# Batch 0's last query block: two key groups mirrored by DMA, and two weight loads put behind waits of the loading queue

## The chip, the cores and the metric

The kernel runs on one core of a Trainium2 chip. The metric is the device time of one execution in microseconds (us), as the median of several runs. A profiled execution has a time of its own, and a span: from its first to its last instruction.

The core has five engines that run side by side, each through its own list of instructions in order: PE (TensorE, matmuls), DVE (VectorE), ACT (ScalarE), POOL (GpSimd) and SP (SyncE). POOL and SP do hardly anything here but issue DMAs. An instruction waits until the semaphores that it needs have their values, and everything behind it on its engine waits with it.

## What is computed

A gated attention without softmax is followed by an MLP mixer, for 8 batches of 3008 rows of 256 channels (z has 64):

```
scores = z @ z.T / 3008                      # 3008 x 3008, symmetric
x      = u * (relu(scores)**2 @ v)
h      = relu(x.T @ w_tok1) @ w_tok2         # over the rows: 3008 -> 256 -> 3008
y      = x + h.T
out    = y + relu(y @ w_ch1) @ w_ch2         # over the channels: 256 -> 1536 -> 256
```

Inputs and output are float32 in memory; the kernel works in bf16 with float32 accumulation.

## The kernel before

**Tiles.** The queries of a batch are cut into 6 blocks (512 columns, the last 448), the keys into 6 groups of 4 tiles of 128. A group of a block, written (b, q, g), is made in two units. A unit is a pair of score matmuls (L440) of 64 rows each, which share the array, into a PSUM pair of banks `sc`; an ACT instruction (L478: relu and scale) into a tile `at`; and a DVE instruction that squares it in place (L486). Later PE multiplies the group with v (L677, called value matmuls here) into accumulators of the block. There are 6 buffers of `at`, and a buffer is written anew only when all that read its last content have finished.

**Mirrors.** Since the scores are symmetric, group (b, g, q) is the transpose of (b, q, g). `direct_block` (L276) says which groups are computed. In batches 1 to 7 that is those with g >= q; the others are mirrors: when both units of (b, q, g) are squared, SP issues one transposing DMA (`flip`, L542) from its `at` into a buffer `fl`, and the value matmuls of (b, g, q) read `fl`. Such an `at` has two users, the block's own value matmuls and the DMA, and its layout is another one (a form 128x4x256 of L478 and L486). In batch 0, MIRROR = 6 makes every group direct: all 36 are computed, and no mirror is made. `key_order` (L286) puts the groups of a block in order.

**Order.** The program is written out by a planner that runs while the kernel is built. It keeps a model of each engine (when it is free, what each step costs), and at each turn writes the step that fits best: a unit's scores, half a group's value matmuls, or a piece of the mixer. What it writes is each engine's fixed order; the chip then keeps to it, whatever the true times are. A step pushed to an engine (`push`, L339) has a room condition. For a mirror that is a free `fl` buffer and `flips_fit` (L536): before the mixer fewer than MIRRORS = 6 buffers of `fl` may be in use; batch 0's six v tiles lie in `fl` buffers too.

**SP** issues all transposes in the order written: of z (`turn_z`, L140 and L144), of u (`turn_u`, L233), of x (`turn_x`, L855) and the mirrors (L546).

**POOL** issues all loads in the order written: z, v, u, w_tok1 (L241), w_tok2 (L251), w_ch1 in two parts (L258) and w_ch2 in two parts (L263). Loads of weights and of u go into buffers of their own and mostly wait for nothing but an old load of their semaphore lane, so POOL runs ahead of the work. Where it must not, `after(column)` (L121) writes a copy of one column of a tile in POOL's order: POOL goes on when that tile is there. `recent[0]` is the tile that was last planned to be written.

**When loads are asked for.** `at_group(n, f)` (L1483) calls f when the planner takes up the n-th group of value matmuls (n counts 6 a block, so block (0,4) begins at 24). The list `items` (L1626) has 24 loads, spread over groups 7 to 33 in its order: v of batch 1, w_tok1, w_tok2, four parts of w_ch, and u (1,0) and u (1,1). So w_tok2's last part is asked for at group 26, w_ch1 at 28 and 29, w_ch2 at 30 and 31. `ask_w_ch` (L1605) also plans the weight sums: when the last part is asked for, four DVE instructions (`sum_weights`, L1611) are pushed that read w_ch2.

## Time and profile before

| | us |
|---|---|
| median of 3 runs | 1116.72 (1116.61 to 1116.90) |
| the profiled execution | 1117.16 |
| its span | 1115.0 |
| PE busy | 1104.5 (99% of the span) |
| DVE busy | 761.9 (68%) |
| ACT busy | 673.0 (60%) |
| POOL busy | 152.2 (14%) |
| block (0,0) ends, (0,1) begins on PE | 24.9 |
| value matmuls of (0,5) begin, with 448 columns | 75.85 |
| batch 0's mixer begins on PE (L900) | 99.65 |

The granted TensorE clock is 0.999 of full speed over the span. A row of the timeline reads: start, duration, engine, line, operation, output and input tiles, how many instructions are merged, and the idle time before them with what ended it. Matmuls overlap in the pipe, so the pace is read from starts, not from durations. [...]

### The profile page before, as it was taken

The numbers are of one execution on the slowest core, as the hardware profiler recorded it, in microseconds if no ns is written. First come the engines' busy times: TensorE is split into PE (matmuls) and PEld (weight loads), VectorE is DVE, ScalarE is ACT, GpSimd is POOL, SyncE is SP. The second block draws the span as 40 slices with busy tenths as digits, with TensorE's granted clock in tenths as the row PEclk, the third lists the DMA queues.
The fourth block names the chain that finished last, engine by engine and source line by source line (L and its number), as shares of the span: only waits on it lengthen the run. The fifth ranks groups of instructions, "written<-read, shape, count | busy, mean of one in ns | idle before, by whom it ended". The sixth has DMA issues, their size and how long they took to land.

```text
span 1115.0 us, 26448 instructions
## 1 busy us (share of the span) xinstructions
PE 1104.5 (99%) x10714; PEld 666.6 (60%) x10788; DVE 761.9 (68%) x1587; ACT 673.0 (60%) x840; POOL 152.2 (14%) x387
## 2 busy tenths in 40 slices
PE   9999999999999999999999999999999999999998
PEld 3555654666447665676545765567654576545676
DVE  7887875676756867568656676566756677655676
ACT  8997585545755467555665456664666636743464
POOL 5401000221002210022100221003210021000000
PEclk9999999999999999999999999999999999999999
DMA  9999485997859988598694997869888697574222
GB/s 173 189 167 185 105 165 110 189 172 145 165 117 193 168 132 183 95 210 168 139 179 96 204 155 153 164 104 219 141 156 153 127 200 145 120 153 84 66 65 80
DMA packets 470411, 165.38 MB, mean 148 GB/s; under 512 B 433232, under 2 KB 448912, under 8 KB 470288
## 3 DMA queue, kind: packets, MB, share of 16 engines
q1 hardware_dynamic: 442432, 130.98, 59.2%
q0 software_dynamic: 27344, 32.32, 20.7%
q8 instruction: 84, 1.38, 0.5%
q14 instruction: 39, 0.32, 0.1%
q10 hardware_dynamic: 512, 0.38, 0.1%
HBM read 65.40 MB, written 24.64 MB: 81 GB/s over the span
## 4 chain that ended last, share of the span: by engine, by line
PE 98%; DMA 1%; issue 0%; POOL 0%; DVE 0%; ACT 0%; POOLq 0%
PE acc L677 42%; PE hp L977 22%; PE f L1096 18%; PE sc L440 6%; PE a_ps L900 4%; PE h_ps L927 4%; PE f L1209 1%; PE first_acc L593 1%; DMA v_sb<-in_v_dram 1%; PE op L1255 0%; PE zp L177 0%; PE up L1589 0%; DVE res L1287 0%; ACT a_sb L909 0%; POOL ident masks.py:199 0%
## 5 line engine op out<-in xcount | busy, mean ns | idle before, releaser
L1024 ACT ACTIVATE h2pre<-hp 128x1024 bf16<-128x1024 f32 (+1 forms) x287 | 283.3, 1005 | 226.6 <-PE hp L977 217.3
L677 PEld LDWEIGHTS <-v_sb 64*128 64x128 bf16 x4418 | 231.2, 94 | 227.8 <-issue 0.9
L677 PE MATMUL acc<-at,v_sb 64*128 64x512 bf16 (+1 forms) x2738 | 337.7, 374 | 0.0
L478 ACT ACTIVATE at<-sc 128x1024 bf16<-128x1024 f32 (+1 forms) x290 | 285.6, 1029 | 69.3 <-PE sc L440 64.1
L486 DVE TENSOR_TENSOR at<-at 128x1024 bf16<-128x1024 bf16 (+1 forms) x290 | 198.0, 686 | 123.5 <-ACT at L478 121.5
L977 PE MATMUL hp<-xT,w_ch_sb 128*128 128x512 bf16 (+1 forms) x1090 | 278.4, 374 | 3.3
L1096 PEld LDWEIGHTS <-h2pre 128*128 128x128 bf16 x3654 | 225.0, 98 | 55.3 <-issue 2.6
L677 PE MATMUL acc<-fl,v_sb 64*128 64x512 bf16 (+1 forms) x1680 | 191.8, 367 | 0.0
L1096 PE MATMUL f<-w_sums,h2pre 128*128 128x128 bf16 x2088 | 184.4, 219 | 0.1
L977 PEld LDWEIGHTS <-w_ch_sb 128*128 128x128 bf16 x1152 | 104.3, 98 | 82.1 <-issue 0.8
L440 PE MATMUL sc<-zT 64*128 64x512 bf16 (+1 forms) x732 | 131.3, 359 | 0.0
L1096 PE MATMUL f<-w_ch_sb,h2pre 128*128 128x128 bf16 x1566 | 128.5, 219 | 0.0
L811 DVE TENSOR_TENSOR cp<-acc,cp 128x512 f32<-128x512 f32 (+1 forms) x94 | 63.5, 675 | 57.1 <-ACT cp L805 56.3
L805 ACT COPY cp<-acc 128x512 f32<-128x512 f32 (+1 forms) x91 | 53.0, 582 | 80.7 <-PE acc L677 80.2
L466 ACT ACTIVATE at<-sc 128x512 bf16<-128x512 f32 (+3 forms) x152 | 54.8, 450 | 36.1 <-PE sc L440 34.0
L1049 DVE TENSOR_TENSOR h2pre<-h2pre 128x512 bf16<-128x512 bf16 (+1 forms) x141 | 56.3, 399 | 18.6 <-PE f L1096 17.7
L1170 DVE TENSOR_TENSOR res<-f,res 128x512 f32<-128x512 f32 (+1 forms) x47 | 30.6, 651 | 49.7 <-PE f L1096 49.7
L440 PEld LDWEIGHTS <-zT 64*128 64x128 bf16 x732 | 39.6, 94 | 41.6 <-issue 3.1
L1051 DVE TENSOR_TENSOR h2pre<-h2pre 128x512 bf16<-128x512 bf16 (+1 forms) x141 | 57.1, 405 | 9.4 <-PE hp L977 0.5
L936 DVE TENSOR_TENSOR xT<-xT,h_ps 128x1024 bf16<-128x1024 bf16 (+1 forms) x48 | 55.8, 1171 | 11.2 <-PE h_ps L927 11.2
L835 DVE TENSOR_TENSOR xT<-cp,uT 128x512 bf16<-128x512 f32 (+1 forms) x94 | 62.4, 664 | 1.2
L1052 DVE TENSOR_TENSOR h2pre<-h2pre 128x512 bf16<-128x512 bf16 (+1 forms) x141 | 57.4, 407 | 4.3
(80 smaller groups left out, 603.0 us busy)
## 6 DMA issues: line engine op xcount, KB each, us to landing
out_dram<-res SPq DMA_DIRECT2D x80, 256.0 KB, 2.5
v_sb<-in_v_dram POOLq DMA_DIRECT2D x40, 256.0 KB, 4.8
ur<-in_u_dram POOLq DMA_DIRECT2D x40, 256.0 KB, 5.4
out_dram<-res SPq DMA_DIRECT2D x24, 128.0 KB, 2.1
w_tok_sb<-in_moe_w_tok_dram POOLq DMA_DIRECT2D x10, 256.0 KB, 10.2
zs<-in_z_dram POOLq DMA_DIRECT2D x35, 64.0 KB, 4.0
at<-at SPq DMA_TRANSPOSE x114, 2.4
fl<-at SPq DMA_TRANSPOSE x105, 4.5
```

Source lines behind the costliest of these rows:

```text
L440: nc.tensor.matmul(sc[:, r, c0:c1], zT[h, k:k + P], zT[h, m + c0:m + c1], start=True, stop=True)
L478: nc.scalar.activation(view, sv, ACT.Relu, scale=inv_S)
L486: nc.vector.tensor_mul(view, view, view)
L677: nc.tensor.matmul(o, vs[blk.b, g][rows, i, dh * P:(dh + 1) * P], rhs, start=(dh, h) not in blk.begun, stop=stop, skip_group_check=True)
L811: nc.vector.tensor_add(cp[:, :W], acc[:, 0, :W], cp[:, :W])
L835: nc.vector.tensor_mul(xT[:, dh, :full * P].rearrange("p (t s) -> p t s", s=P), acc[:, :full * P].rearrange("p (t s) -> p t s", s=P), uT[: ...
L977: nc.tensor.matmul(hp[:, r, :W], w_ch1_sb[:, dc, cc * P:(cc + 1) * P], xT[:, dc, :W], start=(dc == 0), stop=(dc == DT - 1))
L1024: nc.scalar.activation(h2[:, :, :W], hp[:, :, :W], ACT.Relu)
L1049: (3, lambda: nc.vector.tensor_sub(a11, a11, a21)),
L1051: (2, lambda: nc.vector.tensor_sub(a22, a22, a11)),
L1052: (4, lambda: nc.vector.tensor_sub(a12, a12, a22))]
L1096: banked(nc.tensor.matmul(to[:, j, :], lhs[:, j * P:(j + 1) * P], rhs, start=m in (1, 2) and c2 == 0 and j == 0, stop=c2 == CHT // 2 - 1, ...
```

## The change

Groups (0,5,3) and (0,5,4) are no longer computed: they are mirrors of (0,3,5) and (0,4,5), made by two DMAs more. With that, MIRROR goes, and `flips_fit` has a branch of its own for batch 0, since its v tiles alone fill the limit of 6. The list `items` keeps only the two parts of w_ch1, so it has 22 loads, and their groups move: w_tok2's last part to 28, w_ch1 to 29 and 31. The two parts of w_ch2 are asked for at groups 27 and 28, each behind a POOL copy of a column of the tile last planned.

```diff
-    WHOLE, MIRROR = 1, NQ
+    WHOLE = 1
+    FLIPPED = ((5, 3), (5, 4))
...
     def direct_block(b, q, g):
 
-        return g >= q or (b == 0 and g < MIRROR)
+        return g >= q or (b == 0 and (q, g) not in FLIPPED)
...
         n = live["fl"] - live["mix"]
+        if b == 0:
+            return n < ROOM["fl"]
         before_mixer = b < 2 and goal[0] < (0, 0)
...
-    items += [lambda part=part: ask_w_ch(part) for part in range(4)]
+    items += [lambda part=part: ask_w_ch(part) for part in range(2)]
     items += [lambda m=m: load_u(m // NQ, m % NQ) for m in (NQ, NQ + 1)]
     for k, item in enumerate(items):
         at_group(NG + 1 + k * (NQ * NG - 2 * NG + W_LATER) // len(items), item)
+
+    def later_w_ch(part):
+        after(recent[0])
+        ask_w_ch(part)
+
+    for part in (2, 3):
+        at_group((NQ - 2) * NG + part + 1, lambda part=part: later_w_ch(part))
```

Lines of the changed kernel stand 1 to 10 lower in the file: the score matmul is L441, the ACT instruction L479, the square L487, the mirror L549.

## The prediction, before the changed kernel ran

> **What bounds the kernel now.** I read the page first: its busy line and its chain of waits.

> ```profile
> PE 1104.5 (99%) x10714; PEld 666.6 (60%) x10788; DVE 761.9 (68%) x1587; ACT 673.0 (60%) x840; POOL 152.2 (14%) x387
> ...
> PE 98%; DMA 1%; issue 0%; POOL 0%; DVE 0%; ACT 0%; POOLq 0%
> ```

> TensorE (PE) is busy for 99% of the span and is 98% of the chain: a matmul less is time less, and a stall of PE anywhere is time more. The change ends within batch 0: built, both kernels have the same order of PE instructions from batch 0's mixer on. So I asked for PE's waits in the window 0 to 135 us. These are all of them:

> ```profile
> PE wp L198 <- DVE zero L1459: 1.2, 1, 1.2
> PE first_acc L593 <- DMA v_sb<-in_v_dram: 0.9, 1, 0.9
> PE zp L177 <- DVE zr L171: 0.3, 1, 0.3
> PE first_acc L593 <- issue: 0.2, 1, 0.2
> ```

> None lies after 14 us. There is no wait to win back here, only matmuls to leave out, and any new wait is a loss.

> **Removed: eight score matmuls.** Groups (0,5,3) and (0,5,4), written (batch, query block, key group), are two units each, so four pairs of 448-column matmuls. PE's timeline has the pace:

> ```profile
> 75.66 0.37 PE L440 MATMUL sc<-zT 64*128 64x448 bf16 x2
> 75.85 0.94 PE L677 MATMUL acc<-at,v_sb 64*128 64x448 bf16 x8
> ```

> The next instruction starts 0.19 us after a pair does (the 0.37 includes the pipe's length): 4 x 0.19 = **-0.76 us**, all of it on PE. The four activations (0.93 us each) and four squares go too, but ACT and DVE have idle time before their work in this stage (DVE waits 0.2 us for ACT before nearly every square), so they add nothing. The 32 value matmuls that now read the mirror buffer fl instead of at keep their pace: both rows of that shape have a mean of 349 ns.

> **Added: two mirrors on SP, and where they stand in its queue.** SP issues in written order. In the built kernel the mirror of (0,3,5) stands right behind the transposes of x (0,1) and of u (0,4), and those two took this place in time (SP's timeline, before):

> ```profile
> 57.67 4.35 SPq L144 DMA_TRANSPOSE zT<-zs  x1
> 62.11 5.69 SPq L855 DMA_TRANSPOSE x_sb<-xT  x1
> 67.90 3.46 SPq L233 DMA_TRANSPOSE uT<-ur  x1
> 71.45 1.26 SPq L855 DMA_TRANSPOSE x_sb<-xT  x1
> ```

> The source at tile of (0,3,5) is squared by about 47 us, but SP is far behind: an issue that takes 1.26 us when the DMA engines are free takes 3.5 to 5.7 us here. Why: the DMA view of 55 to 60 us.

> ```profile
> q0 software_dynamic: 642, 0.86, 95.0%
> q1 hardware_dynamic: 642, 0.16, 24.3%
> ```

> POOL's loads (q0) and SP's transposes (q1) get one packet each in turn, and POOL's are far longer. From 72 to 75 us, with POOL's loads over, transposes alone move 2966 packets in 3 us, 990 a us against 642 / 5 = 128:

> ```profile
> q1 hardware_dynamic: 2966, 0.74, 109.4%
> ```

> **The wait that this adds.** A mirror holds its at tile until its DMA has landed. The built kernel puts group (0,4,1) into the tile of (0,3,5): its first activation waits for that mirror's landing, and the next-but-one score matmul needs the PSUM pair which that activation empties. ACT's row for it in the kernel before, and PE's row for that matmul:

> ```profile
> 58.86 1.09 ACT L478 ACTIVATE at<-sc 128x1024 bf16<-128x1024 f32 x1
> ```
> ```profile
> 60.11 0.40 PE L440 MATMUL sc<-zT 64*128 64x512 bf16 x2
> ```

> The activation gives the pair up at 59.95 and the matmul starts at 60.11: no slack. Every us that the mirror lands after 58.86 is a us of PE, with squares and copies behind ACT and all of PE's queue behind that matmul.

> **When it lands.** The change keeps POOL's last loads back. Its fifth w_tok2 part is issued at 46.59 as before (the row's landing is 10.4 us), so q0 runs dry at 57.0, where before it ran on to about 70. Then:

> ```profile
> fl<-at SPq DMA_TRANSPOSE x1, 3.7
> ```

> - By SP's issues: after the transpose that ends at 57.58, three issues of about 1.26 us and gaps bring it to 61.5; the mirror lands 3.7 us after its issue starts: 65.2.
> - By packets: from 57.0 to 73.5 us q1 moved 5119, some 760 of them of the next x transpose, so 4360 lie ahead; the mirror's 128 x 2048 bf16 are 2048 packets of 256 B. (4360 + 2048) / 990 = 6.5: 63.5 at the earliest.

> I take 64.8, nearer to SP's issues since each has its row, a little sooner as SP will be less behind once q0 is dry. Stall: 64.8 - 58.86 = **+5.9 us**. Ends: 63.5 gives 4.6; 66.0 (with DMA pauses like the 0.4 us one at 75 us) gives 7.1.

> **PE's pace after such a stall.** Two rows of PE:

> ```profile
> 1.20 3.13 PE L198 MATMUL wp<-zero 128*128 128x512 bf16 x7 [1.20 <-DVE zero L1459]
> ...
> 8.70 0.60 PE L593 MATMUL first_acc<-at,v_sb 128*128 128x512 bf16 x2 [0.86 <-DMA v_sb<-in_v_dram]
> ```

> The first seven matmuls take 3.13 us where the usual 0.215 each makes 1.5: starting cold cost 1.6 us. After a pause of 0.86 us the pace is full. No pause in between is in the trace, so the cost is 0 to 1.6; 5.9 us is seven times the harmless one, so I take the cold start, **+1.6**, and keep 0 as the other end.

> [...]

> **Moved: the second channel weights.** They are said to be asked for later. In POOL's queue they move forward: to groups 27 and 28 from 30 and 31, both ahead of w_ch1, the first ahead of w_tok2's last part too. Later in time is only their wait: POOL copies a column of at tiles (0,4,4) and (0,5,0), squared at about 68.6 and 70 in the kernel before, so near 75 and 76 now. Behind the waits stand w_tok2's last part, w_ch1 and two u loads. Before, that traffic took from 57.0 to 70.0, so all lands by about 90. Who needs it: the weight sums on DVE, at 94.30 before and some three us earlier in the new order, plus 5.1 for the shift: 96; w_ch1 at 107.71 on PE; u's transpose, for a gate at 99. Cover 6 us or more: I count it as nothing. Without it, DVE would stall with squares behind.

> The second mirror, of (0,4,5), follows three issues after the first, so lands near 69; its tile is wanted by (0,5,1) at about 71 + 5.9. Nothing. The other reordering in (0,5) and (1,0) has no row; PE waited nowhere there, so I bound it at 0 to 0.5.

> **Sum.** Against the profiled execution (1117.16; span 1115.0): 1117.16 - 0.76 + 5.9 + 1.6 = 1123.9. That execution is 0.44 above the median of 1116.72, so **1123.4 us**. The terms' ends: -0.76 + 4.6 + 0 = +3.8 (1120.6) to -0.76 + 7.1 + 1.6 + 0.5 = +8.4 (1125.2).

> **Rivals.**
> 1. The mirror is in time: lands by 58.9, PE never stops, only the matmuls go: 1115.96, inside 0.2% (2.2 us, about what a measurement of this kernel can tell from no change). For: traffic is lighter after 57. Against: SP would have to be at the mirror by 55.2, and at 55.09 it was three transposes before it. It decides at a landing of 58.86. Chance 0.13.
> 2. A part of it: SP catches up by some 3 us more than I count, the stall is 2 to 4 us and PE keeps its pace: 1118.0 to 1120.0. 0.08.
> 3. POOL's waits put a needed load onto the path: the w_ch2 half lands after 96, DVE holds its squares, PE up to 3 us more: 1124 to 1127. Against: 6 us of cover. 0.04.
> 4. The loads aren't held back (the copied tile is long ready): then the mirror keeps its old place, 71.45 + 3.7 = 75.2, a stall of 16.3: 1133.9. Against: the tile copied is (0,4,4). 0.02.
> 5. Something else is won (less DMA traffic from 57 to 70): PE has no wait there to give back. 0.02.

> The main case has 0.71. Faster by over 0.2%: rival 5 and 0.01 for measurement, 0.03. Same: the rest of rival 1 and half of rival 2 (under 1118.95), 0.16. Slower: 0.81. The range runs from 1118.0 to 1127.0: the main case with both ends of its terms and rivals 2 and 3; outside lie rivals 1, 4 and 5, 0.17.

> **What would show it.** PE's waits up to 135 us: a new one of 4.6 to 7.1 us at L441's score matmul near 60 us, released by ACT's L479 activation, which itself waits for the DMA fl<-at. In SP's timeline the first fl<-at is issued near 61.5. Matmuls at double length for some 3 us after the stall, or not. POOL's w_ch2 issues near 75 and 77, no DVE wait at the weight sums. L440's 448-column matmuls 24 to 16. I am wrong if the first mirror lands before 59, or if ACT's wait is there but PE has none.

## The result, and the profile after

The median after the change is 1123.42 us (7 runs, 1121.95 to 1126.02) against 1116.90 us before (7 runs on the same chip, 1116.61 to 1121.6). The ratio is 1.0052, with a 95% interval of 1.0029 to 1.0075: slower by half a per cent. The profiled execution took 1123.75 us, its span is 1121.9 us. The ratios below too are made from runs that stood side by side, so one need not be the quotient of two medians.

The page after, busy line and chain by engine:

```profile
PE 1110.0 (99%) x10780; PEld 666.7 (59%) x10780; DVE 760.4 (68%) x1582; ACT 670.5 (60%) x837; POOL 153.7 (14%) x389
...
PE 97%; ACT 1%; DVE 1%; DMA 0%; SPq 0%; issue 0%; ACTq 0%
```

The averages hide it: PE is still busy 99% of the span. (The instruction counts of the two pages can't be compared, since records go missing; those of one tile can: 732 matmuls into `sc` before, 724 after.) Queue q1, SP's transposes and stores, moved 446592 packets in the place of 442432, two mirrors of 2080. PE's waits over the whole span, and under them ACT's largest in the window of 40 to 100 us:

```profile
PE sc L441 <- ACT at L479: 6.6, 1, 6.6
PE wp L198 <- DVE zero L1462: 1.2, 1, 1.2
```
```profile
ACT at L479 <- DMA fl<-at: 6.8, 1, 6.8
```

One new wait in 1122 us. Its history on SP, with the lines of the changed kernel (L858 is the transpose of x, L549 a mirror; a row of SPq is the time in which SP was busy with issuing, and tells nothing of the landing):

```profile
49.76 7.09 SPq L140 DMA_TRANSPOSE zT<-zs  x2
56.93 1.18 SPq L144 DMA_TRANSPOSE zT<-zs  x1
58.21 1.26 SPq L858 DMA_TRANSPOSE x_sb<-xT  x1
59.56 1.26 SPq L233 DMA_TRANSPOSE uT<-ur  x1
60.91 1.34 SPq L549 DMA_TRANSPOSE fl<-at  x1
```

Until 57 us two issues take 7.09 us, afterwards each takes 1.2 to 1.3: the last of POOL's first wave of loads landed at 57.04. The first mirror, issued at 60.91, landed at 64.77. ACT's timeline and PE's at the same place:

```profile
64.85 2.86 ACT L479 ACTIVATE at<-sc 128x1024 bf16<-128x1024 f32 x3 [6.75 <-DMA fl<-at]
```
```profile
65.93 0.61 PE L441 MATMUL sc<-zT 64*128 64x512 bf16 x2 [6.57 <-ACT at L479]
66.31 1.94 PE L680 MATMUL acc<-at,v_sb 64*128 64x512 bf16 x8
68.01 0.66 PE L441 MATMUL sc<-zT 64*128 64x512 bf16 x2
68.44 2.69 PE L680 MATMUL acc<-at,v_sb 64*128 64x512 bf16 x16
70.96 0.39 PE L441 MATMUL sc<-zT 64*128 64x512 bf16 x2
```

ACT starts 0.08 us after the landing, PE 1.08 us after ACT. Then look at the distances: eight matmuls (four row pairs) take 68.01 - 66.31 = 1.70 us, where they took 0.86 in the profile before (60.33 to 61.19). The windows of the trace show why (columns: window, length, busy time with instructions of PE, PEld, DVE, ACT and POOL, then the granted clock):

```profile
62.00:63.00 1.00, 0.00 (x0) 0.00 (x0) 0.00 (x0) 0.00 (x0) 0.00 (x0) 1.00 1.03 236
63.00:64.00 1.00, 0.00 (x0) 0.00 (x0) 0.00 (x0) 0.00 (x0) 0.00 (x0) 0.60 1.26 286
...
68.00:70.00 2.00, 2.00 (x12) 0.89 (x10) 1.72 (x3) 1.02 (x1) 0.00 (x0) 0.50 0.30 69
70.00:71.00 1.00, 1.00 (x12) 0.48 (x10) 1.00 (x3) 0.00 (x0) 0.00 (x0) 0.99 0.00 0
```

PE went idle at 59.36, the granted clock fell to 0.50 at 63.20, 3.8 us later, and it stayed there for the first 4.1 us of work, to 70.03. From the score matmul at the stall to the second one behind it the kernel before needed 63.14 - 60.11 = 3.03 us; here it is 70.96 - 65.93 = 5.03: half clock cost 2.0 us.

The spans add up: 1115.0 + 6.57 (stall) + 2.0 (half clock) - 0.76 (matmuls) - 0.9 = 1121.9. The last term is no part of the change: PE's wait for `v_sb` near 8 us, 0.9 us in the profile before, isn't in this execution.

### The profile page after: what moved, and what is told of

It reads as the page before. It is cut to its first block, busy times and chain, and to the rows that moved or that the text cites. A ratio compares the mean times of both kernels' runs of the same rounds, so it can differ in the third digit from the quotient of the medians.

```text
span 1121.9 us, 26510 instructions
## 1 busy us (share of the span) xinstructions
PE 1110.0 (99%) x10780; PEld 666.7 (59%) x10780; DVE 760.4 (68%) x1582; ACT 670.5 (60%) x837; POOL 153.7 (14%) x389
## 3 DMA queue, kind: packets, MB, share of 16 engines
q1 hardware_dynamic: 446592, 132.03, 60.0%
## 4 chain that ended last, share of the span: by engine, by line
PE 97%; ACT 1%; DVE 1%; DMA 0%; SPq 0%; issue 0%; ACTq 0%
PE acc L680 41%; PE hp L980 22%; PE f L1099 18%; PE sc L441 6%; PE a_ps L903 4%; PE h_ps L930 4%; PE f L1212 1%; ACT at L479 1%; PE first_acc L596 1%; DVE at L487 0%; PE op L1258 0%; DMA fl<-at 0%; PE wp L198 0%; PE first_acc L198 0%; SPq L233 0%
## 5 line engine op out<-in xcount | busy, mean ns | idle before, releaser
L479 ACT ACTIVATE at<-sc 128x1024 bf16<-128x1024 f32 (+1 forms) x286 | 281.9, 1031 | 77.0 <-PE sc L441 61.9
L487 DVE TENSOR_TENSOR at<-at 128x1024 bf16<-128x1024 bf16 (+1 forms) x286 | 196.0, 688 | 131.3 <-ACT at L479 128.5
L980 PE MATMUL hp<-xT,w_ch_sb 128*128 128x512 bf16 (+1 forms) x1152 | 281.7, 375 | 0.0
L680 PE MATMUL acc<-fl,v_sb 64*128 64x512 bf16 (+1 forms) x1712 | 195.6, 367 | 0.0
L441 PE MATMUL sc<-zT 64*128 64x512 bf16 (+1 forms) x724 | 130.2, 360 | 6.6 <-ACT at L479 6.6
L1052 DVE TENSOR_TENSOR h2pre<-h2pre 128x512 bf16<-128x512 bf16 (+1 forms) x141 | 56.4, 400 | 18.9 <-PE f L1099 18.0
L441 PEld LDWEIGHTS <-zT 64*128 64x128 bf16 x724 | 39.4, 94 | 48.6 <-issue 10.3
L1054 DVE TENSOR_TENSOR h2pre<-h2pre 128x512 bf16<-128x512 bf16 (+1 forms) x141 | 57.3, 406 | 9.1
L838 DVE TENSOR_TENSOR xT<-cp,uT 128x512 bf16<-128x512 f32 (+1 forms) x94 | 62.5, 665 | 1.3
L123 POOL CAST mark<-at 128x1 f32<-128x1 bf16 x14 | 3.9, 277 | 430.2 <-DVE at L487 420.2
## 6 DMA issues: line engine op xcount, KB each, us to landing
w_tok_sb<-in_moe_w_tok_dram POOLq DMA_DIRECT2D x10, 256.0 KB, 10.4
```

Of the source, the lines that this page charges most:

```text
L441: nc.tensor.matmul(sc[:, r, c0:c1], zT[h, k:k + P], zT[h, m + c0:m + c1], start=True, stop=True)
L479: nc.scalar.activation(view, sv, ACT.Relu, scale=inv_S)
L487: nc.vector.tensor_mul(view, view, view)
L680: nc.tensor.matmul(o, vs[blk.b, g][rows, i, dh * P:(dh + 1) * P], rhs, start=(dh, h) not in blk.begun, stop=stop, skip_group_check=True)
L838: nc.vector.tensor_mul(xT[:, dh, :full * P].rearrange("p (t s) -> p t s", s=P), acc[:, :full * P].rearrange("p (t s) -> p t s", s=P), uT[: ...
L980: nc.tensor.matmul(hp[:, r, :W], w_ch1_sb[:, dc, cc * P:(cc + 1) * P], xT[:, dc, :W], start=(dc == 0), stop=(dc == DT - 1))
```

## The experiments

The theory: **a hidden deadline.** The first mirror reads the `at` tile that group (0,4,1) is to be written into, and it lands late, because SP's transposes share the DMA engines with POOL's loads (642 packets each from 55 to 60 us in the profile before). The rivals: the late weights cost something; the second mirror does; the wait is for something else than the tile.

**The late weights alone**, `FLIPPED` emptied:

```diff
-    FLIPPED = ((5, 3), (5, 4))
+    FLIPPED = ()
```

> Only the second half of the change: no mirrors in batch 0, but w_ch2 behind the two POOL waits. Theory (the first mirror, late in SP's queue, keeps its at tile from ACT and so stops PE): no mirror, no stall: 1116.9 us, within 2 of the kernel before; PE has no wait over 0.5 us between 20 and 135 us. Rival (the late loads cost the time: weight sums or w_ch1 come late): about 1123, with DVE or PE waiting for w_ch2 or w_ch1.

Measured: 1116.62 us (10 runs), ratio 0.9993 (0.9983 to 1.0003). The profile has no PE wait but the 1.2 us at the start. The last part of w_ch landed at 80.43 us. Weights that are asked for late cost nothing.

**Both mirrors alone**, with the loads as before the change:

```diff
-    items += [lambda part=part: ask_w_ch(part) for part in range(2)]
+    items += [lambda part=part: ask_w_ch(part) for part in range(4)]
...
-    for part in (2, 3):
-        at_group((NQ - 2) * NG + part + 1, lambda part=part: later_w_ch(part))
```

> Only the first half of the change: both mirrors, but all four w_ch parts asked for as before. Theory: POOL's loads run on to about 70 us, so SP reaches the first mirror near 71 and it lands near 75; ACT wants its tile near 58.9: a stall of about 16 us, plus 2 for the half clock, less 0.8: 1134 us (1131 to 1137). Rival 1 (the POOL waits are what costs): about 1116. Rival 2 (two mirrors more on the DMA engines cost a fixed amount, wherever they stand): about 1123, as with the whole change.

Measured: 1134.3 us (4 runs), ratio 1.0151 (1.0125 to 1.0176). PE's wait and SP's row of the first mirror:

```profile
PE sc L441 <- ACT at L479: 15.0, 1, 15.0
```
```profile
69.68 1.66 SPq L549 DMA_TRANSPOSE fl<-at  x1
```

With the channel weights back in it, the first wave of loads ends at 68.18 us in the place of 57.04; the mirror lands at 73.63, and PE waits 15.0 us. So the late weights don't cost, they **save**: they take 11 us off the price of the mirrors.

**One mirror at a time.** First the second mirror alone, `FLIPPED = ((5, 4),)`:

> The whole change, but only group (0,5,4) is a mirror; (0,5,3) is computed. Theory: this mirror's tile is wanted near 71 us and it lands near 68: no PE wait, and half of the matmuls are saved: 1116.5 us. Rival (each mirror costs about half of the loss, by DMA traffic or by the order of blocks (0,5) and (1,0)): about 1120.

Measured: 1116.53 us (10 runs), ratio 0.9992 (0.998 to 1.0004). The mirror was issued at 64.24 and landed at 68.14, and PE waited for nothing but the 1.2 us at the start. Then the first alone, `FLIPPED = ((5, 3),)`:

> The change with the first mirror alone, group (0,3,5); (0,4,5) is computed as before. Theory: the whole stall is the first mirror's: PE's wait of 6 to 7 us and 2 us of half clock as in the whole change, and 0.38 us less saved: 1123.8 us (1122.3 to 1125.5). Rival (the two mirrors delay each other, or the second keeps PE waiting too): 1118 to 1121 us.

Measured: 1125.35 us (4 runs), ratio 1.0074 (1.006 to 1.0089). PE's wait at the same matmul is 6.44 us, and the mirror landed at 64.71. (This execution has a wait of 0.9 us at 178.8 us as well.) The loss is the first mirror's, all of it.

**More `at` tiles.** If ACT waits for the tile, more buffers move the deadline and leave the landing alone. Seven tiles, one `fl` less:

```diff
-    ROOM = {"at": 6, "fl": 15, "xT": 9, "v": NG, "us": 3, "res": RES}
+    ROOM = {"at": 7, "fl": 14, "xT": 9, "v": NG, "us": 3, "res": RES}
```

> The change with seven at tiles in the place of six (fl has 14 in the place of 15). Theory (the wait is for the reuse of the at tile): the tile of (0,3,5) is wanted one round of the six later, by about 1.85 us, so ACT's wait for fl<-at and PE's behind it are 4.7 us in the place of 6.6, with half clock after it still: 1121.5 us (1120.5 to 1122.5). Rival (the wait is for something else that comes from the mirror, its fl tile or the order on SP): 6.6 us of wait as before and 1123.4 us.

Measured: 1123.61 us (4 runs), ratio 1.0067 (1.0054 to 1.008). **The theory's number missed**, and the rival's was met. The trace says why: the deadline did move, but the landing moved too, to 66.21, since the first wave of loads ended at 58.55. So the question was put again, with nine and with eight tiles (`fl` 12 and 13), and with nine tiles and a third mirror (`FLIPPED` with `(4, 3)` added):

> The change with nine at tiles in the place of six (fl has 12 in the place of 15). The run with seven left the time where it was, but there the mirror landed 1.4 us later and its tile was wanted only 1.3 us later, so it told nothing. Theory (ACT waits because it reuses the tile that the mirror still reads): with nine the tile of (0,3,5) is wanted seven of ACT's groups later, near 66 us, and a mirror that lands between 64.8 and 66.2 us is in time; no wait for it over 0.5 us, no half clock, and what the four pairs of score matmuls save is left: 1116.2 us (1115.5 to 1118.0). Rival (the wait is for something else that comes with the mirrors, the fl tile's readers or SP's order): PE's wait of 6 to 7 us stays and it takes 1123.4 us.

> The change with eight at tiles (fl has 13). Theory: the tile of (0,3,5) is wanted four groups later than with six, near 62.8 us; the mirror lands between 64.8 and 66.2 us, so ACT waits for 2.0 to 3.4 us, PE 1.8 to 3.2 us, and half clock follows for 0 to 1.6 us: 1119.0 us (1117.5 to 1121.0), between the runs with six and with nine. Rival: as with six, 1123.4 us.

> Nine at tiles and a third mirror, group (0,3,4), which takes two more pairs of score matmuls away, 0.43 us. Theory: the tile that it reads is wanted six groups after that of (0,3,5), near 72 us, and its transpose stands third after that one on SP, so it lands near 69 us: no wait, 1115.8 us (1115.0 to 1117.5). Rival (SP's queue has no room for one more): a wait of ACT for fl<-at of 2 us or more near 72 us or at batch 1's first mirrors near 93 us, and 1118 to 1124 us.

Measured: nine, 1123.83 us (12 runs), ratio 1.0044 (1.0008 to 1.0079); eight, 1130.52 us (10 runs), 1.0091 (1.0057 to 1.0125); nine and a third mirror, 1118.41 us (12 runs), 1.0015 (0.997 to 1.0061). All three times missed what I expected. They spread widely on that chip, as did those of the kernel before (1116.2 to 1135.4), so the waits tell more than the times. ACT's row at the mirror's landing with seven, eight, nine, and nine with a third mirror:

```profile
66.30 2.85 ACT L479 ACTIVATE at<-sc 128x1024 bf16<-128x1024 f32 x3 [7.05 <-DMA fl<-at]
```
```profile
68.31 1.94 ACT L479 ACTIVATE at<-sc 128x1024 bf16<-128x1024 f32 x2 [6.71 <-DMA fl<-at]
```
```profile
66.49 6.17 ACT L479 ACTIVATE at<-sc 128x1024 bf16<-128x1024 f32 x7 [2.27 <-DMA fl<-at]
```
```profile
65.11 6.25 ACT L479 ACTIVATE at<-sc 128x896 bf16<-128x896 f32 x7 [1.11 <-DMA fl<-at]
```

Start less wait is the deadline, and the mirror's landing is known from its own row:

| `at` tiles | loads' first wave over | mirror landed | tile wanted | ACT's wait | PE's |
|---|---|---|---|---|---|
| 6 (the change) | 57.04 | 64.77 | 58.10 | 6.75 | 6.57 |
| 6, first mirror alone | 57.02 | 64.71 | 58.17 | 6.63 | 6.44 |
| 7 | 58.55 | 66.21 | 59.25 | 7.05 | 6.92 |
| 8 | 61.38 | 68.23 | 61.60 | 6.71 | 5.82 |
| 9 | 56.70 | 66.41 | 64.22 | 2.27 | 1.81 |
| 9, third mirror | 55.88 | 65.03 | 64.00 | 1.11 | 0.6 |

The deadline moves with the number of tiles, and in every row ACT starts 0.08 to 0.09 us after the landing. That is what the rival (a wait for something else) can't give. What failed was my picture of the landing, which I held to be fixed: it moved by up to 3.5 us between these kernels, and not with the loads' end alone: with nine tiles the loads ended 0.3 us earlier than after the change, yet the mirror landed 1.6 us later. In that execution q1 moved 38 packets between 62.5 and 64.5 us, where it moved 2242 in the same window after the change. With eight tiles q0 moved 25 packets between 58.5 and 61.0 us, where it moved 684 in 5 us (50 to 55) after the change. So the traffic nearly stopped for some 2 us in both; what stopped it was not settled. Nor did nine tiles come for free. The run with nine has a second wait of PE, far from the change, for DVE's instruction at L1166, which writes the tile `res`:

```profile
PE f L1099 <- DVE res L1166: 3.1, 1, 3.1
PE acc L680 <- ACT at L479: 1.8, 1, 1.8
```

It stands at 936 us, and half clock follows it (granted 0.72 and 0.78 in the windows from 935 to 942 us). With eight tiles four such waits make 5.3 us. Fewer `fl` tiles were my guess for their cause. That wasn't tried alone, and the profile of nine tiles with a third mirror, which has the same 12 `fl` tiles, shows no such wait, so the cause is open.

**Earlier mirror.** The other half of the theory is that the mirror is late because of the loads. So they are held back: the six parts of w_tok2 go behind a POOL copy of group (0,4,1)'s tile.

```diff
+        if 2 * NG <= k < 3 * NG:
+            continue
...
+    def later_w_tok2(c):
+        if c == 0:
+            after(recent[0])
+        ask_w_tok2(c)
+
+    for c in range(NG):
+        at_group((NQ - 2) * NG + 1 + c // 3, lambda c=c: later_w_tok2(c))
```

> The whole change, and all six w_tok2 parts too are asked for later, behind a POOL copy of the tile of (0,4,1). Theory: POOL's queue runs dry near 48 us instead of 57, SP catches up, the first mirror lands at 58 to 59, as ACT wants its tile at 58 to 59: a PE wait of 0 to 1 us, too short for the half clock: 1116.2 us (1115.6 to 1117.5). Rival (loads held back cost time): over 1123, since more is held back.

Measured: 1115.9 us (10 runs, 1114.85 to 1120.58), ratio 0.9985 (0.9967 to 1.0003). Eight of ten runs lie between 1114.9 and 1117.0, the other two at 1119.4 and 1120.6. The profiled execution is the slowest: there the loads ended at 51.16, the mirror landed at 61.89, 2.9 us earlier than after the change, and PE still waited 3.4 us. The other nine executions have no profile. By their times the stall is gone or short in most of them, and what remains is about the 0.76 us saved; the mirror's time would then vary from one execution to the next by more than its margin. Then three parts of w_tok1 were put behind the copy too, which now stands before them:

```diff
-        if 2 * NG <= k < 3 * NG:
+        if NG + 3 <= k < 3 * NG:
             continue
...
+    def later_w_tok1(c):
+        if c == 3:
+            after(recent[0])
+        load_w_tok1(c)
...
+    for c in range(3, NG):
+        at_group((NQ - 2) * NG + 1, lambda c=c: later_w_tok1(c))
```

> As hold_tok2, and the last three parts of the first token weights are also put behind the copy that waits for the tile of group (0,4,1). Theory (the mirror is late because the POOL loads share the 16 DMA engines with SP's transposes, packet by packet, until they run out): with about 1.2 us less of loads ahead per held part the loads run out near 45 us, the first mirror lands near 55 to 56 us, ahead of the 57.9 us at which its tile is wanted, also in an execution whose loads started late; no wait of ACT for fl<-at, no wait of PE behind it, 1115.9 us (1114.9 to 1117.0) with less spread than hold_tok2 (1114.9 to 1120.6). Rival (a mirror just takes its time wherever it stands, or the held weights are missed later): a PE wait of 3 us or more for ACT at L479, or a new one for DVE, and 1119 to 1124 us.

> hold_more with a third mirror, group (0,3,4). It removes two more pairs of 512-column score matmuls, 0.43 us. Theory: its tile is wanted again near 66 us, its transpose stands in SP's queue behind x(0,2) and lands before that, as the loads have run out by then: 1115.4 us (1114.5 to 1116.6), no PE wait. Rival (SP's queue is now what is late, because each mirror holds it for about 3.5 us): a PE wait for ACT at L479 of 2 to 8 us near 66 us, 1118 to 1124 us.

Measured: 1118.64 us (12 runs, 1116.84 to 1125.26), ratio 1.003 (1.0013 to 1.0047); with the third mirror 1126.15 us (6 runs), 1.0084 (1.0059 to 1.011). **Both missed, with times near the rivals':** there are new waits of PE for ACT at L479, though not where the rivals put them, and neither the first mirror nor a missing weight is behind them. In the first of the two runs (its profile is of a fast execution, 1117.54; four others took 1123.8 to 1125.3, and what those waited for is not shown) the mirror was issued at 51.16 and landed at 54.86: in time, as the theory said. But all the held loads now ran from 61 to 90 us, and there batch 1's first two mirrors stand in SP's queue. SP's row of these two, without and with the third mirror:

```profile
80.71 13.50 SPq L549 DMA_TRANSPOSE fl<-at  x2
```
```profile
79.53 23.96 SPq L549 DMA_TRANSPOSE fl<-at  x2
```

After the change their issues took 4.90 and 1.75 us. The second one's tile was late in turn: ACT waited 4.26 us until 97.00 (it landed at 96.90), PE 1.86. With the third mirror these two landed at 104.06 and 105.70, and PE waited

```profile
PE sc L441 <- ACT at L479: 12.5, 1, 12.5
```

again for a mirror that still read its tile, at another place, 106.9 us. The backlog of loads had not gone; it had been moved onto the next transposes. That is not all of it: in this last run q0 and q1 moved 742 and 754 packets from 80 to 87.5 us, 194 GB/s in all, and only 86 and 1048 from 87.5 to 96, 49 GB/s. Why the traffic slowed is open. No version here beats the kernel before by more than its interval: the best, with w_tok2 held, reaches 0.9985. Putting the first mirror ahead of the transposes of x and u in SP's order, with the loads left alone, was not tried.

## Why the prediction was right

**The bound, and the saved matmuls.** PE has no other new wait, and 724 score matmuls are left of 732. Right. The saving itself is too small to measure alone: with the second mirror alone the median is 0.3 us lower (0.38 worked out), and the interval is 1.3 us to either side. The -0.76 fits the sum of the spans.

**The mirror's place and landing.** Issued at 60.91 (61.5 said), landed at 64.77 (64.8). Of the two ways to work it out, SP's issues and the packets, the first was right in kind: once q0 was dry SP took exactly the three short issues, from a start 0.7 us earlier than taken (56.85 for 57.58). The packets' number was nearly right (6544 moved from 57.04 to the landing, 6408 counted), their pace was not: from 58.5 to 61.0 us, while SP issued one transpose after the other, q1 moved 1273, 509 a us and not the 990 counted on. q0's end, 57.0 said, was 57.04.

**The stall: the mechanism was right, the size was 6.57 in the place of 5.9.** The landing was right and the deadline wasn't: I took ACT's due time, 58.86 (58.10 found), from the profile before, which had 0.9 us of waiting at 8 us in it that this execution hasn't. What the stall takes out of the whole is 6.57 - 0.9 = 5.7 us. A deadline read from one execution carries that execution's early waits with it.

**The cold start: +1.6 said, 2.0 found**, outside the 0 to 1.6 that I allowed. I had the size from the kernel's first seven matmuls, and PE was at half pace for longer here: 4.1 us in which it worked. In the trace's clock record the clock stood at 0.50 for 6.83 us, the last of the idle time among them, and fell 3.8 us after PE had gone idle. Other runs have other times. With seven tiles PE's last matmul ended at 60.45, the clock fell at 62.93, 2.5 us later, and PE began again at 67.37:

```profile
62.00:63.00 1.00, 0.00 (x0) 0.00 (x0) 0.00 (x0) 0.00 (x0) 0.00 (x0) 0.97 0.86 196
63.00:64.00 1.00, 0.00 (x0) 0.00 (x0) 0.00 (x0) 0.00 (x0) 0.00 (x0) 0.50 0.72 161
```

With w_tok2 held the pause was 3.42 us, PE worked at full clock from 63.05 for about a microsecond, and only then the clock fell:

```profile
63.00:64.00 1.00, 0.95 (x10) 0.53 (x11) 0.74 (x2) 1.00 (x2) 0.14 (x1) 0.99 0.74 167
64.00:66.00 2.00, 2.00 (x13) 0.84 (x11) 2.00 (x4) 1.85 (x2) 1.34 (x3) 0.50 1.05 238
```

The two deviations (+0.67 and +0.4) and the missing 0.9 us cancel to 0.2, so the predicted 1123.4 is nearer than its terms were, by luck.

**The late weights: nothing.** Right. w_ch2 was issued at 76.31 and 78.17 (75 and 77 said), the held loads had landed by 93.2 (90), the sums on DVE started at 98.1.

**The rivals.** A mirror in time would have needed a landing before 58.1; it was 6.7 us later. The fourth rival (loads not held back: 1133.9) is the run with both mirrors alone, 1134.3, though the stall was 15.2 us on ACT, not 16.3. Nothing was won elsewhere.

## What to carry to other kernels

A DMA that reads a rotating buffer gives that buffer's next writer a deadline: look up which instruction gets the tile next, and compare its time with the landing, not with the issue. Work that is asked for later doesn't leave the DMA queues, it meets whatever is there then (here batch 1's first two mirrors: 13.50 us on SP with the loads held, 6.74 after the change), so ask what it will stand in front of. On an engine that is busy 99% of the time, 0.76 us saved doesn't pay for one pause of 3.1 us or more, which in these runs cost the pause itself and then half of the 3.1 to 6.0 us of work done at a clock of 0.50, 1.6 to 3.0 us.
